# Deferring the tanh and gates of the last two feed-forward chunks into the attention stage

## The chip, the cores and the metric

One core of a Trainium2 chip. The metric is the device time of one execution in microseconds.

## The reference, cut to what matters

```python
xn = layernorm(x)                                   # x: 2048 x 448
q  = xn @ wq                                        # 16 heads of 256
s  = softmax(q k^T / 16) v, heads joined, @ wo      # k, v: the last 512 cached positions, 8 kv heads
g  = silu((gelu(xn @ w_gate) * (xn @ w_up)) @ w_down)   # feed-forward width 1792
out = x + s * g
```

The kernel works on four chunks of 512 rows. It computes the gates `g` of all chunks first, stores them to memory, and fetches them again when the attention output of each chunk is finished. SiLU is written as x * (1 + tanh(x/2)) with factors folded elsewhere, so it can use tanh beside the softmax's exp.

## The kernel before

Every operation is recorded into one list; each engine gets its operations in the recorded order, and a helper inserts the semaphore waits that buffers and data demand. So the place of a line in the program decides its place in an engine's queue. The down product of chunks 1 to 3 is a Strassen-like scheme of seven half-size products (`down7`): PE makes the products, DVE adds them up, ACT takes tanh, DVE multiplies.

```python
def down7(c, banks, g, b_g, order=(3, 6, 5, 4, 2, 1), then=None):
    B1, B4, B6, B7, B5, B3 = banks
    ...
    product(0, B1, A(0, 0))
    act(U2, bank[B1][:, 0:D], ACT.Copy, (b_ps[B1],), bU2, scale=F)
    for j in order:
        product(j, *what[j], j != 1)
    if then:
        then()                        # chunk 2: the differences that chunk 3 needs, on DVE
    plus(U2, bU2, B6, U2, bU2)        # plus: one DVE pass, bank * F + V
    plus(U3, bU3, B7, U2, bU2)
    sums(0, B4, U3, bU3)              # sums: a plus, then tanh on ACT
    sums(1, B5, U3, bU3)
    gate(0, 1, 0)                     # gate: (tanh + 1) * sum on DVE
    plus(U2, bU2, B5, U2, bU2)
    act(Cs[2][0][:, :], bank[B1][:, 0:D], ACT.Copy, (b_ps[B1],), (Cs[2][1],), scale=F)
    sums(2, B3, U2, bU2)
    gate(1, 1, 1); store(1)
    sums(3, None, None, None)
    gate(2, 0, 1)
    ...                               # gate(3), store(0)
```

The attention loop interleaves with it. `s_mm` puts a head's four score products on PE, their exponentials on ACT, their normalisation on DVE (`pn`) and their transposes on the DMA queue of SP (`pT`). `pv` is the product with the values, two heads later.

```python
for m in range(NS):                   # heads of all chunks
    if m in groups:                   # query products for the next 4, 8 or 6 heads, two heads at a time
        ...
        if m == Q0 and p == 0:        # Q0 = 4: the second query group
            K.reuse(b_kT[2:] + b_va[3:])
        if p == 0 and m in (Q0, Q0 + QS):
            for g in range(2, 7) if m == Q0 else (7,): load_k(g)
            for g in range(3, 6) if m == Q0 else (6, 7): load_v(g)
    s_mm(m)
    if m == 0: down7(2, ...)()        # after the first head's scores
    if m == 1:
        down7(3, ...)()               # after the second head's scores
        ...
        for t in range(NG2): load_g2(t)                                # POOL: first gate tiles
        for t in range(NXR): dma("pool", xr[:, t, :], x_view[:, t, :], ...)   # POOL: first input tiles
    if len(late) == LAG: pv(late.pop(0))
```

The scores use the banks AB0 to AB3, the value products BB0 to BB3, and `down7` borrows AB2, AB3 and all of BB.

The softmax here doesn't subtract the row's maximum and nothing guards it: scores larger than these inputs give would overflow.

## Time and profile before

| | before |
|---|---|
| time, median | 546.23 us |
| span of the profiled run | 544.4 us |
| PE busy | 537.4 us, 99% |
| PE idle in 114 to 156 us | 2.2 us |

The lines are shown in the prediction. Two habits of reading help here. A line of the waits view is "engine line waited for: us in total, times, longest us". And on PE, compare the starts of equal groups rather than their ends: a group of eight attention matmuls is listed with 1.89 us, but the next group starts 1.73 us after it. The Trainium skill warns of matmul busy time too: "Perfetto Trace Analysis", section "Identifying the Most-Contended Engine", calls it no good measure of how close a kernel is to the roofline, because PE's instructions are pipelined.

### The profile page before, as it was taken

To read this page: it belongs to the slowest core of one execution; us is meant where nothing else is said; L and a number is where in the kernel's file an instruction comes from. 1 tells how busy PE (TensorE), PEld (TensorE's weight loads), DVE (VectorE), ACT (ScalarE), POOL (GpSimd) and SP (SyncE) were. 2 spreads that over 40 slices of the span, in tenths; PEclk is the share of its full clock that TensorE was granted. 3 is DMA by queue.
4 is the path that set the end of the run, shared out by engine and by line. 5 is a ranking of instruction groups with operands and counts; after the bars stand their busy time and mean duration, and the time that the engine had idled before them with its cause. 6 is when DMAs were issued, how large, how long until landed. Compare 5 with 4: busy or idle time off the path is not lost.

```text
span 544.4 us, 10795 instructions
## 1 busy us (share of the span) xinstructions
PE 537.4 (99%) x4106; PEld 305.8 (56%) x4106; DVE 376.1 (69%) x823; ACT 313.9 (58%) x784; POOL 39.5 (7%) x78
## 2 busy tenths in 40 slices
PE   9999999999999999999999999999999999999997
PEld 5554457458644444894444469644444984444487
DVE  6673885799757757944775786467667934776775
ACT  5433854873648858306875870388488216876820
POOL 1130400000100000003001000020000003001010
PEclk9999999999999999999999999999999999999999
DMA  9569272912398758302771680056456402783631
GB/s 283 132 185 130 48 138 71 293 40 53 106 177 196 144 115 155 79 1 67 165 152 33 152 155 1 18 139 155 95 102 151 68 1 75 162 151 84 151 51 34
DMA packets 171459, 61.36 MB, mean 113 GB/s; under 512 B 154960, under 2 KB 168272, under 8 KB 171408
## 3 DMA queue, kind: packets, MB, share of 16 engines
q1 hardware_dynamic: 167632, 51.39, 44.4%
q0 software_dynamic: 3008, 8.72, 7.1%
q8 instruction: 32, 0.52, 0.4%
q10 hardware_dynamic: 768, 0.57, 0.3%
q14 instruction: 19, 0.16, 0.1%
HBM read 19.76 MB, written 3.67 MB: 43 GB/s over the span
## 4 chain that ended last, share of the span: by engine, by line
PE 90%; DVE 5%; ACT 2%; issue 1%; DMA 1%; DVEq 0%; ACTq 0%
PE bank L390 89%; ACT p L836 2%; DVE wt L384 1%; DVE pn L843 1%; DMA pT<-pn 1%; DVE actTh L557 1%; PE bank L507 1%; DVE qT L821 0%; DVE sd L384 0%; DVE rden L840 0%; DVE cd L608 0%; DVE tmp L608 0%; ACT th L381 0%; DVE actTh L384 0%; PE bank L488 0%
## 5 line engine op out<-in xcount | busy, mean ns | idle before, releaser
L836 ACT ACTIVATE p<-bank 128x512 f32<-128x512 f32 x256 | 150.4, 596 | 26.3 <-DVE pn L843 24.0
L390 PE MATMUL bank<-kT,qT 128*128 128x512 bf16 x512 | 121.6, 380 | 1.1 <-ACT p L836 1.1
L390 PE MATMUL bank<-pT,va 128*128 128x512 bf16 x512 | 120.8, 379 | 0.0
L843 DVE TENSOR_SCALAR pn<-p,rden 128x512 bf16<-128x512 f32 x256 | 113.0, 484 | 9.5 <-DMA pT<-pn 5.1
L390 PE MATMUL bank<-xnT,wq 64*128 64x512 bf16 x768 | 94.9, 377 | 0.5 <-DVE oTh L861 0.5
L390 PEld LDWEIGHTS bank<-kT,qT 128*128 128x128 bf16 x512 | 49.0, 98 | 63.8 <-issue 3.4
L390 PE MATMUL bank<-xnT,wgu 64*128 64x512 bf16 (+2 forms) x768 | 84.2, 351 | 0.1
L390 PEld LDWEIGHTS bank<-pT,va 128*128 128x128 bf16 x512 | 49.8, 98 | 60.7 <-DMA pT<-pn 1.6
L381 ACT ACTIVATE qT<-bank 128x512 bf16<-128x512 f32 x76 | 44.1, 596 | 55.0 <-PE bank L390 53.4
L821 DVE CAST qT<-bank 128x512 bf16<-128x512 f32 x52 | 34.9, 690 | 51.4 <-PE bank L390 51.4
L390 PEld LDWEIGHTS bank<-xnT,wq 64*128 64x128 bf16 x768 | 36.6, 94 | 47.0 <-ACT p L836 2.0
L390 PEld LDWEIGHTS bank<-xnT,wgu 64*128 64x128 bf16 x768 | 37.1, 95 | 36.9 <-issue 0.6
L840 DVE RECIPROCAL rden<-rsum 128x2 f32<-128x2 f32 x128 | 21.2, 166 | 48.3 <-ACT p L836 48.2
L836 ACT ACTIVATION_READ_ACCUMULATOR p<-bank 128x1 f32 x256 | 51.7, 202 | 0.0
L381 ACT ACTIVATE gl<-bank 128x512 bf16<-128x512 f32 x56 | 33.2, 597 | 29.5 <-PE bank L390 27.0
L390 PE MATMUL bank<-wt,sr 128*128 128x224 f16 x512 | 49.7, 259 | 0.0
L390 PEld LDWEIGHTS bank<-wt,sr 128*128 128x128 f16 x512 | 49.1, 98 | 0.0
L381 ACT ACTIVATE xnT<-bank 128x224 bf16<-128x224 f32 (+2 forms) x12 | 4.4, 400 | 72.2 <-PE bank L390 70.9
L861 DVE TENSOR_SCALAR oTh<-bank 128x512 f16<-128x512 f32 x62 | 42.4, 683 | 0.0
L381 ACT ACTIVATE oTh<-bank 128x512 f16<-128x512 f32 x66 | 38.9, 589 | 4.6 <-PE bank L390 4.6
L390 PE MATMUL bank<-wt,oTh 128*128 128x224 f16 x384 | 38.3, 259 | 0.3 <-ACT oTh L381 0.3
L390 PEld LDWEIGHTS bank<-wt,oTh 128*128 128x128 f16 x384 | 36.7, 98 | 1.8 <-ACT oTh L381 1.1
(77 smaller groups left out, 407.9 us busy)
## 6 DMA issues: line engine op xcount, KB each, us to landing
wtb<-in_A_wo_dram POOLq DMA_DIRECT2D x4, 896.0 KB, 10.8
wq<-in_A_wq_dram SPq DMA_DIRECT2D x2, 1536.0 KB, 7.3
va<-in_A_v_cache_dram SPq DMA_DIRECT2D x8, 256.0 KB, 4.1
pT<-pn SPq DMA_TRANSPOSE x128, 2.8
xr<-in_A_x_dram POOLq DMA_DIRECT2D x15, 112.0 KB, 2.3
wd<-in_B_w_down_dram SPq DMA_DIRECT2D x1, 1568.0 KB, 7.6
g<-g_all POOLq DMA_DIRECT2D x14, 112.0 KB, 2.3
out_dram<-xr POOLq DMA_DIRECT2D x12, 112.0 KB, 2.1
```

Of the source, the lines that this page charges most:

```text
L381: K.op("act", lambda e, o=o, i=i: e.activation(o, i, func, scale=scale), reads, writes)
L384: K.op(eng, lambda e: e.tensor_tensor(o, x, y, op), reads, writes)
L390: ins = e.matmul(o, lhsT=l, rhs=r, start=st, stop=sp, skip_group_check=True)
L507: ins = e.matmul(bank[b][:, 0:w], lhsT=gl[:, 0, 0:P], rhs=gl[:, 0, 0:w], start=True, stop=True)
L557: K.op("dve", lambda e: e.tensor_tensor(o[:, c % 2, f, :], bank[b + 1], gl[:, s, :], ALU.mult), (b_ps[b + 1], b_gl[s]), (b_actT[c % 2][f],))
L821: K.op("dve", lambda v, s=s, b=b: v.tensor_copy(qT[:, s, 1, :], bank[b + 1]), (b_ps[b + 1],), (b_qT[s][1],))
L836: K.op("act", lambda e, b=b, r=r, z=z: e.activation(p32[:, z, :], bank[b], ACT.Exp, scale=att_scale, accum_out=rsum[:, r:r + 1]), (b_ps[b] ...
L840: K.op("dve", lambda e, r=r: e.reciprocal(rden[:, r - 1:r + 1], rsum[:, r - 1:r + 1]), b_rsum[r - 1:r + 1], b_rden[r - 1:r + 1])
L843: K.op("dve", lambda e, r=r - 1 + t, z=(n - 1 + t) % NP32, y=y, t=t: e.tensor_scalar(pn[:, y, t, :], p32[:, z, :], rden[:, r:r + 1], None, ...
L861: K.op("dve", lambda v, i=i, b=b: v.tensor_scalar(oTh[:, i, :], bank[b], WS, None, op0=ALU.mult), (b_ps[b],), (b_oT[i],))
```

## The change

The intent: take the tanh and gates of chunks 2 and 3 out of the way of the first heads' exponentials. The sums stay where they are and are kept in buffers. Chunk 2's tanh and gates run while PE makes chunk 3's products, chunk 3's run between pairs of the second query group. To free memory for the kept sums, chunks 2 and 3 get one tanh buffer instead of two, key and value loads are split by what each has to wait for, and POOL's first five loads move behind chunk 3's gates. One product of chunk 2 changes its turn, and chunk 1's tanh and gates now follow all its sums. `K.reuse` says that the buffers named take over memory of others, so that their first writer waits for the last users of those. Cut to its core:

```diff
+            outs = [(x[:, :], [bx]) for x, bx in Cs[:2]] + [(U3, bU3)] + [(Cs[2][0][:, :], [Cs[2][1]])]
             ...
             sums(0, B4, U3, bU3)
             sums(1, B5, U3, bU3)
-            gate(0, 1, 0)
+            act(outs[3][0], bank[B1][:, 0:D], ACT.Copy, (b_ps[B1],), outs[3][1], scale=F)
             plus(U2, bU2, B5, U2, bU2)
-            act(Cs[2][0][:, :], bank[B1][:, 0:D], ACT.Copy, (b_ps[B1],), (Cs[2][1],), scale=F)
             sums(2, B3, U2, bU2)
-            gate(1, 1, 1)
-            store(1)
-            sums(3, None, None, None)
-            gate(2, 0, 1)
-            def end():
-                gate(3, 0, 0)
-                store(0)
+            def end(*qs):
+                for q in qs: tanh(q)
+                for q in qs:
+                    gate(q)
+                    if q in (1, 3): store((0, 1)[q == 1])
             return end
 ... second query group
+                    if m == Q0 and p < 3:
+                        K.reuse(b_kT[2:6] + b_va[3:4] if p == 0 else b_kT[6:] + b_va[4:] if p == 2 else [])
+                        for k in ((2, 3, 4, 5), (), (6,))[p]: load_k(k)
+                        if p == 0: load_v(3)
+                        if p < 2:
+                            gates3(2 * p); gates3(2 * p + 1)
+                        else:
+                            load_v(4); load_v(5)
+                            K.reuse([b for y in b_xr for b in y])
+                            for t in range(NG2): load_g2(t)
+                            for t in range(NXR): dma("pool", xr[:, t, :], x_view[:, t, :], (), b_xr[t])
 ... after the first and second head's scores
-                    down7(2, ..., g2w, b_g2w, then=lambda: [sum_act(3, k) for k in range(4)])()
+                    gates2 = down7(2, ..., g2w, b_g2w, (3, 4, 6, 5, 2, 1), lambda: [sum_act(3, k) for k in range(4)])
-                    down7(3, ..., (3, 4, 2, 5, 6, 1))()
+                    gates3 = down7(3, ..., (3, 4, 2, 5, 6, 1), lambda: [gates2(q) for q in range(4)])
 ... (buffer places and the old load lines cut)
```

More of the change, by code (lines that the diff above doesn't have):

```diff
@@ L344, in bass_recurrent_scan__sliding_block_cached__geglu_ffn__prompt_kernel @@
         a_v, a_th = b_va[3].lo, at2 + 3 * TD
-        dn[2] = places(2, [(2, a_v), (1, a_v + SD), (0, b_pT[2][0].lo)], [a_v + 2 * SD, b_pT[1][0].lo, b_pn[2].lo], [a_th, b_pT[1][0].lo + CD])
-        dn[3] = places(3, [], [a_v + 2 * SD, b_pT[2][0].lo, b_pn[2].lo], [a_th, b_pT[2][0].lo + CD])
+        dn[2] = places(2, [(2, a_v), (1, a_v + SD), (0, b_pT[2][0].lo)],
+                       [a_v + 2 * SD, b_pT[2][0].lo, b_pT[2][0].lo + CD], [a_th])
+        dn[3] = places(3, [], [a_v + 2 * SD, a_v + SD, a_v + SD + CD], [a_th])
         dn[3][0].update({i: (actTh[:, 0, 0:NH, i * HC // 2:i * HC // 2 + HC], b_actT[0][0:NH]) for i in (0, 2)})
@@ L609, in plus, with tanh, gate @@
                     out=o, in0=bank[b][:, 0:D], scalar=F, in1=V, op0=ALU.mult, op1=ALU.add), [b_ps[b]] + bV, bo)
+            outs = [(x[:, :], [bx]) for x, bx in Cs[:2]] + [(U3, bU3)] + [(Cs[2][0][:, :], [Cs[2][1]])]
             def sums(q, b, V, bV):
-                x, bx = Cs[(0, 1, 0, 2)[q]]
-                if b is not None:
-                    plus(x[:, :], [bx], b, V, bV)
-                y, by = Ts[q % 2]
-                act(y[:, :], x[:, :], ACT.Tanh, (bx,), (by,), scale=0.5)
-            def gate(q, r, n):
+                plus(*outs[q], b, V, bV)
+            def tanh(q):
+                x, bx = outs[q]
+                y, by = Ts[q % len(Ts)]
+                act(y[:, :], x, ACT.Tanh, bx, (by,), scale=0.5)
+            def gate(q):
+                r, n = ((1, 0), (1, 1), (0, 1), (0, 0))[q]
                 two = lambda x: x.rearrange("p (t d) -> p t d", t=2)
-                (x, bx), (y, by) = Cs[(0, 1, 0, 2)[q]], Ts[q % 2]
+                (x, bx), (y, by) = outs[q], Ts[q % len(Ts)]
                 K.op("dve", lambda e: e.scalar_tensor_tensor(
-                    out=g[r][:, :, n * N2:(n + 1) * N2], in0=two(y[:, :]), scalar=1.0, in1=two(x[:, :]),
-                    op0=ALU.add, op1=ALU.mult), (by, bx), b_g[2 * r:2 * r + 2])
+                    out=g[r][:, :, n * N2:(n + 1) * N2], in0=two(y[:, :]), scalar=1.0, in1=two(x),
+                    op0=ALU.add, op1=ALU.mult), [by] + bx, b_g[2 * r:2 * r + 2])
             def store(r):
@@ L633, in down7 @@
                 product(j, *what[j], j != 1)
+            K.reuse([b for _, b in Cs + Ts])
             if then:
@@ L639, in down7 @@
             sums(1, B5, U3, bU3)
-            gate(0, 1, 0)
+            act(outs[3][0], bank[B1][:, 0:D], ACT.Copy, (b_ps[B1],), outs[3][1], scale=F)
             plus(U2, bU2, B5, U2, bU2)
-            act(Cs[2][0][:, :], bank[B1][:, 0:D], ACT.Copy, (b_ps[B1],), (Cs[2][1],), scale=F)
             sums(2, B3, U2, bU2)
-            gate(1, 1, 1)
-            store(1)
-            sums(3, None, None, None)
-            gate(2, 0, 1)
-            def end():
-                gate(3, 0, 0)
-                store(0)
+            def end(*qs):
+                for q in qs:
+                    tanh(q)
+                for q in qs:
+                    gate(q)
+                    if q in (1, 3):
+                        store((0, 1)[q == 1])
             return end
@@ L790, in bass_recurrent_scan__sliding_block_cached__geglu_ffn__prompt_kernel @@
                 if DOWN_AT[n + 1] == 1:
-                    down7(1, (cur[0], cur[0] + 1, cur[1], cur[1] + 1, nxt[0], nxt[0] + 1),
-                          (g2x[:, 0:2, :], g2x[:, 2:4, :]), b_g2x)()
+                    end = down7(1, (cur[0], cur[0] + 1, cur[1], cur[1] + 1, nxt[0], nxt[0] + 1),
+                          (g2x[:, 0:2, :], g2x[:, 2:4, :]), b_g2x)
+                    end(0, 1)
+                    end(2, 3)
                     cur, nxt = (nxt[1], cur[1]), (cur[0], nxt[0])
@@ L999, in bass_recurrent_scan__sliding_block_cached__geglu_ffn__prompt_kernel @@
                         sum_act(2, 2 + p)
-                    if m == Q0 and p == 0:
-                        K.reuse(b_kT[2:] + b_va[3:])
-                    if p == 0 and m in (Q0, Q0 + QS):
-                        for g in range(2, 7) if m == Q0 else (7,):
-                            load_k(g)
-                        for g in range(3, 6) if m == Q0 else (6, 7):
-                            load_v(g)
+                    if m == Q0 and p < 3:
+                        K.reuse(b_kT[2:6] + b_va[3:4] if p == 0 else b_kT[6:] + b_va[4:] if p == 2 else [])
+                        for k in ((2, 3, 4, 5), (), (6,))[p]:
+                            load_k(k)
+                        if p == 0:
+                            load_v(3)
+                        if p < 2:
+                            gates3(2 * p)
+                            gates3(2 * p + 1)
+                        else:
+                            load_v(4)
+                            load_v(5)
+                            K.reuse([b for y in b_xr for b in y])
+                            for t in range(NG2):
+                                load_g2(t)
+                            for t in range(NXR):
+                                dma("pool", xr[:, t, :], x_view[:, t, :], (), b_xr[t])
+                    if m == Q0 + QS and p == 0:
+                        load_k(7)
+                        load_v(6)
+                        load_v(7)
                     if end and p:
@@ L1017, in bass_recurrent_scan__sliding_block_cached__geglu_ffn__prompt_kernel @@
                 if m == 0:
-                    down7(2, (BB[0], BB[1], AB[2], AB[3], BB[2], BB[3]), g2w, b_g2w,
-                          then=lambda: [sum_act(3, k) for k in range(4)])()
-                    K.reuse(b_pT[1] + b_pn[2:])
-                else:
-                    K.reuse(dn[3][3])
-                    down7(3, (BB[1], BB[0], AB[2], AB[3], BB[2], BB[3]), g2w, b_g2w, (3, 4, 2, 5, 6, 1))()
+                    gates2 = down7(2, (BB[0], BB[1], AB[2], AB[3], BB[2], BB[3]), g2w, b_g2w, (3, 4, 6, 5, 2, 1),
+                                   lambda: [sum_act(3, k) for k in range(4)])
+                else:
+                    gates3 = down7(3, (BB[1], BB[0], AB[2], AB[3], BB[2], BB[3]), g2w, b_g2w, (3, 4, 2, 5, 6, 1),
+                                   lambda: [gates2(q) for q in range(4)])
+                    K.reuse(b_pT[2])
                 if m == LAG - 1:
-                    K.reuse(b_pT[2] + b_pn[2:])
                     K.reuse(b_oT + [b for y in b_qT[:QS - Q0] for b in y])
                     assert not CASTS and not SUMS
-                    K.reuse([b for y in b_xr for b in y])
-                    for t in range(NG2):
-                        load_g2(t)
-                    for t in range(NXR):
-                        dma("pool", xr[:, t, :], x_view[:, t, :], (), b_xr[t])
             if len(late) == LAG:
```

## The prediction

> **What bounds the kernel now.** I read the page first, then the waits of the matmul engine inside the stage that the diff touches, and last that stage's timelines for PE, ACT and DVE side by side. The page settles how large the answer can be:
>
> ```profile
> span 544.4 us, 10795 instructions
> PE 537.4 (99%) x4106; PEld 305.8 (56%) x4106; DVE 376.1 (69%) x823; ACT 313.9 (58%) x784; POOL 39.5 (7%) x78
> PE 90%; DVE 5%; ACT 2%; issue 1%; DMA 1%; DVEq 0%; ACTq 0%
> ```
>
> PE shows only 7.0 us of idle time in the whole span, and the change removes no matmul. Cut into five stretches, the same trace puts 1.2 us of that idle time into the first 20 us, nothing into 20 to 114, 2.2 us into 114 to 156 (39.81 busy of 42), practically nothing into 156 to 500 and 3.2 us into the tail after 500. The diff acts on the third stretch: the sums, tanh and gates of chunks 2 and 3, wedged between the first attention heads.
>
> In that stretch PE waited for two things:
>
> ```profile
> PE bank L390 <- ACT p L836: 1.7, 3, 0.9
> PE bank L390 <- DVE oTh L861: 0.5, 1, 0.5
> ```
>
> The idle column understates the loss, because a matmul's modelled end includes the time its result takes to come out. Starts against the normal spacing are the better ruler. The PE timeline:
>
> ```profile
> 122.14 1.50 PE L390 MATMUL bank<-wdt,actTh 128*128 128x224 f16 x14
> 124.17 1.51 PE L390 MATMUL bank<-wdt,actTh 128*128 128x224 f16 x14 [0.53 <-ACT p L836]
> ...
> 143.74 1.89 PE L390 MATMUL bank<-pT,va 128*128 128x512 bf16 x8
> 146.51 1.76 PE L390 MATMUL bank<-kT,qT 128*128 128x512 bf16 x6 [0.89 <-ACT p L836]
> 148.53 0.61 PE L390 MATMUL bank<-kT,qT 128*128 128x512 bf16 x2 [0.26 <-ACT p L836]
> 148.97 1.89 PE L390 MATMUL bank<-pT,va 128*128 128x512 bf16 x8
> 150.79 0.82 PE L390 MATMUL bank<-xnT,wq 64*128 64x512 bf16 x6
> ...
> 155.37 0.82 PE L390 MATMUL bank<-xnT,wq 64*128 64x512 bf16 x6 [0.51 <-DVE oTh L861]
> ```
>
> Undisturbed, 14 gate matmuls take 1.35 us (124.17 to the next group at 125.52), eight attention matmuls 1.73 us (142.01 to 143.74), and a query matmul 0.108 us (18 of them, 156.24 to 158.18). So the losses are: at 124.17, 2.03 - 1.35 = 0.68; at 146.51, 2.77 - 1.73 = 1.04; within the scores after it, 2.46 - 1.73 = 0.73; the next head's product 1.82 - 1.73 = 0.09; and 36 query matmuls from 150.79 to 155.37, 4.58 - 3.89 = 0.69. **Sum: 3.23 us.** That is what is to be had.
>
> Why PE waited there is in the ACT timeline:
>
> ```profile
> 144.77 1.11 ACT L381 ACTIVATE th<-cd 128x448 f32<-128x448 f32 x2 [0.98 <-DVE cd L608]
> 145.79 0.58 ACT L836 ACTIVATE p<-bank 128x512 f32<-128x512 f32 x1
> ```
>
> The scores of the third head began at 142.01, so their first bank was full by about 142.5; ACT reached its exponential only at 145.79, because four tanh stood before it in ACT's queue, with gaps of 4.10 and 0.98 us in which they waited for DVE sums. The fourth head's scores need those banks back. The 5.55 us transfer in the chain of waits is the other half: the transposed weights issued at 148.18 shared the DMA with five loads that POOL issued from 147.69 to 150.4, against a median landing of 2.8 us; DVE then sat 2.07 us, and its copy out of a bank came late for the query product at 155.37.
>
> **What the Trainium skill says.** "PSUM — Partial Sum Buffer", section "Engine vs sequencer instructions": the ACT and DVE queues are strictly first in, first out. The trace agrees: the exponential's input stood ready some 3.3 us while it waited behind tanh. "ScalarE: Activation LUTs", section "Table sets: the hidden batching unit": tanh sits in the same table set as exp, so spreading tanh among exponentials should cost no table load. The trace agrees: the one load (1.28 us) of this stage is at 113.77, and none stands between tanh and exp later. "VectorE: DVE Perf Modes", section "Why PSUM operands drop a tier": a PSUM operand leaves fp32 at the plain rate. The sums and the gates both take 622 ns for 448 columns whether they read PSUM or not, so moving a gate does not change its cost. "DMA: Bandwidth & Descriptors", section "Issuing engines are not separate DMA queues": loads from POOL and SP share the 16 engines; the 5.6 us landing against 2.8 agrees.
>
> **The change part by part.** No matmul, sum, tanh or gate is added or removed: eight sums-and-copies, four tanh (about 0.53 us each) and four gates (0.62) per chunk as before. Only places, buffers and transfers move.
>
> 1. Product order of chunk 2. The product whose left side is an already finished difference now runs before the one that needs the last score bank. Its input was finished at 120.6 and its bank evacuated by 119.7, so it can start at 123.49; the one that waited then starts at 124.84, after the exponential that held it to 124.17. Gain 0.68 us on PE. The chunk-3 differences on DVE overwrite an input of that product, now free at about 126.2 instead of 125.5; DVE gets there at 126.2, so this is even or 0.1 us.
>
> 2. Chunk 2's tanh and gates leave the place before the second head's exponentials. These, which ran at 135.03, can begin at about 130.8, as soon as their scores exist. The six sums run on DVE from 129.5 to 133.2 unbroken, then the four normalisations of the second head to about 135.7. Freed banks are enough for what follows.
>
> 3. They then run behind chunk 3's first copy on ACT. One tanh buffer makes them a ping-pong: tanh 0.66 to the gate's start, gate 0.67 to the next tanh, 1.33 us a round (142.26 to 142.92 in the trace gives the first). Four rounds from 135.0 end at about 140.3. This is 5.3 us in which DVE is held, and chunk 3's sums can start only then.
>
> 4. Chunk 3's sums: 140.3 to 144.0 by six sums of 0.55 to 0.65. PE, 0.68 ahead, starts the third head's scores at 141.3. Their third and fourth banks are needed at 142.2 and 142.6; the sums release them at about 141.0 and 141.6. That fits with about 1.0 us to spare. ACT is then free, so the exponentials start at about 142.0, the fourth waits for a normalisation at 144.6, and the next scores (PE at 144.8, last bank needed at 146.1) find the bank read by 145.2. So 1.04 + 0.73 + 0.09 = 1.86 us come back.
>
> 5. Chunk 3's tanh and gates go between query pairs. A pair takes PE 3.03 us. ACT holds 1.25 us of copies and two tanh of 1.11, DVE 1.34 and two gates of 1.16: 2.4 and 2.5 us, both under 3.03, and the banks are wanted a pair later. No cost.
>
> 6. POOL's five loads move behind the gates, out of the transposes' way. The bank copy that held the query product should end near 150.5, needed at 152.1: 0.69 us back.
>
> Sum: 0.68 + 1.86 + 0.69 = 3.23, and 546.23 - 3.23 = 543.0. I leave 0.1 us for small slips: **543.1 us**, 0.6% less. After the query group PE has no idle time in which a shift could be lost. Chunk 1, where all tanh now follow all sums, ends its gates about 1 us later, but DVE has gaps of 0.9 us there, and PE waited for nothing between 20 and 114: zero.
>
> **The rivals.** First, the ping-pong delays the chunk-3 sums: if a round costs 1.6 instead of 1.33 us, the sums slip 1.1 us and the scores' third bank comes late; the stall at 146.5 would move to 142 and part of the 1.86 us would be lost, time near 543.8. For it: tanh and gate wait for each other through one buffer. Against it: the measured 0.66 and 0.67 already contain the semaphore times.
>
> Second, the transfers only collide elsewhere. The key loads now start near 151 instead of 156, but the last of them and the five POOL loads wait for gates at about 157 to 158 and are in flight to about 163, when the fifth head's transposes are issued. Should those land in 5.5 us again, DVE waits about 0.5 us, perhaps twice; the cost on PE would be 0 to 0.7 us. Against it: right after the key loads, at 166.72, the transposes of before went out with no wait on PE.
>
> Third, PE's idle time was harmless slack and ACT or DVE sets the pace of the attention that follows, giving the gain back. ACT's period there is 3.45 us per head (164.32 to 167.83 to 171.28), PE's 3.46. That is close, and it speaks for caution, but the pace of PE is unbroken from 156 to 500, so a start 3.2 us earlier should end 3.2 us earlier. Full loss would leave 546.2.
>
> **Range and chances.** The ceiling of the gain is 3.23 us plus perhaps 0.5 that I overlooked, so 542.5 is the low end. Rivals one and two together would cost up to 1.5 us: the high end is 544.6. Two per cent is 10.9 us, more than all idle time of PE, so faster by that much is ruled out by the count of matmuls; slower by that much would take a serial wait that no view suggests.
>
> **What would show it.** Right: PE busy stays 537 us while the span drops to about 541.2; the waits of PE on exponentials and on the bank copy in 114 to 156 are gone; the fifth head's scores start near 160.4 instead of 163.67; second-head exponentials begin near 131; the transposes of the third head land in about 3 us. Wrong at step 1: a gap before the fourth product group remains. Wrong at step 3 or 4: a wait of PE on a sum (or on the bank copy) appears near 142. Wrong at step 6: a transpose with 5 us landing near 163 and a DVE wait behind it. A time above 545 would mean that the lost time was taken back within the attention stage.

## The result and the profile after

Four executions of each: 544.34 us median (543.65 to 544.61) against 546.21 us (544.96 to 546.40). Ratios here are from the runs of both kernels in the same rounds, and not quite the ratio of the quoted medians: 0.9969, 95% interval 0.9951 to 0.9986. The time fell by 1.9 us, where the prediction had 3.1: inside its range, within 2% as forecast, but with little more than half of the gain.

The page after, the lines that answer to those of before:

```profile
span 542.4 us, 10788 instructions
PE 536.5 (99%) x4106; PEld 305.8 (56%) x4106; DVE 375.8 (69%) x823; ACT 313.8 (58%) x784; POOL 39.6 (7%) x78
PE 93%; ACT 2%; DVE 2%; DMA 2%; issue 1%; ACTq 0%
```

The span is 2.0 us shorter at the same work; DVE's share of the chain that ended last fell from 5% to 2%, while the share of DMA rose from 1% to 2%. PE's waits from 112 to 185 us after the change, the whole answer:

```profile
PE bank L391 <- DMA pT<-pn: 0.9, 1, 0.9
```

The two waits of before (on exponentials, on a bank copy) are gone. A new one stands there: the product with the values waits for transposed weights. The PE timeline shows where:

```profile
123.35 1.50 PE L391 MATMUL bank<-wdh,sd 128*128 128x224 f16 x14
124.69 1.50 PE L391 MATMUL bank<-wdt,actTh 128*128 128x224 f16 x14
...
142.90 1.89 PE L391 MATMUL bank<-pT,va 128*128 128x512 bf16 x8
144.63 1.89 PE L391 MATMUL bank<-kT,qT 128*128 128x512 bf16 x8
146.35 1.89 PE L391 MATMUL bank<-pT,va 128*128 128x512 bf16 x8
148.18 0.82 PE L391 MATMUL bank<-xnT,wq 64*128 64x512 bf16 x6
...
160.37 1.90 PE L391 MATMUL bank<-kT,qT 128*128 128x512 bf16 x8
...
167.29 1.89 PE L391 MATMUL bank<-kT,qT 128*128 128x512 bf16 x8
170.08 1.90 PE L391 MATMUL bank<-pT,va 128*128 128x512 bf16 x8 [0.91 <-DMA pT<-pn]
```

Up to 160.37 every group starts at its normal spacing: the fifth head's scores begin at 160.37, where the prediction said "near 160.4 instead of 163.67". Then 2.79 us pass between two starts where 1.73 is normal: 1.06 us are given back. Comparing the starts of equal query groups along the whole run, the lead over the kernel before is 3.30 us in the second query group (0.14 of it from ahead of the first head), 2.22 in the third (189.84 against 192.06), 2.07 at 342.78, 1.85 at 382.93 and 2.04 at 483.60. So most of what is missing is lost in one place, near 168; some 0.4 us more goes between there and 383, and 0.2 comes back. The traces show where: at 275.44 and 363.18 a product with the values starts 0.14 and 0.22 us late after a weight load that waited 0.5 us for a transpose, and at 466.55 the kernel before has the same.

Two more views of the profile after show what happened near 168. First the DMA issues of POOL, then a line of DVE, and the landing times of the transposes from 160 to 180 us (issue to landing, minimum, median, maximum):

```profile
161.74 1.10 POOL L376 DMA_DIRECT2D g<-g_all  x2 [94.00 <-DMA g_all<-g]
162.83 1.83 POOL L376 DMA_DIRECT2D xr<-in_A_x_dram  x3
```

```profile
169.44 0.88 DVE L850 TENSOR_SCALAR pn<-p,rden 128x512 bf16<-128x512 f32 x2 [2.00 <-DMA pT<-pn]
```

```profile
DMA to landing us min/median/max: 2.7/2.7/5.8
```

And from the chain that ended last, the transfer that PE waited for:

```profile
165.21 4.82 DMA pT<-pn
```

POOL's five loads go out from 161.7 to 164.7, as soon as chunk 3's gates are stored. The fifth head's transposes are issued from 163.5. The longest lands 5.8 us after its issue, where 2.7 is the median, and the one that PE needs after 4.82 us. DVE waits for a buffer of weights, and PE for the weights. It is the collision that the kernel before had at 148, moved to 163.

### The profile page after: what moved, and what is told of

It reads as the page before. It is cut to its first block, busy times and chain, and to the rows that moved or that the text cites. A ratio compares the mean times of both kernels' runs of the same rounds, so it can differ in the third digit from the quotient of the medians.

```text
span 542.4 us, 10788 instructions
## 1 busy us (share of the span) xinstructions
PE 536.5 (99%) x4106; PEld 305.8 (56%) x4106; DVE 375.8 (69%) x823; ACT 313.8 (58%) x784; POOL 39.6 (7%) x78
## 4 chain that ended last, share of the span: by engine, by line
PE 93%; ACT 2%; DVE 2%; DMA 2%; issue 1%; ACTq 0%
PE bank L391 92%; ACT p L843 2%; DMA pT<-pn 2%; DVE pn L850 1%; PE bank L508 1%; DVE rden L847 0%; ACT qT L382 0%; PE bank L489 0%; ACT oTh L382 0%; ACT xnT L382 0%; DVE xnT L385 0%; DVE xr L385 0%; DVE gl L421 0%; DVE epst L422 0%; ACTq L155 0%
## 5 line engine op out<-in xcount | busy, mean ns | idle before, releaser
L391 PE MATMUL bank<-pT,va 128*128 128x512 bf16 x512 | 120.9, 379 | 1.0 <-DMA pT<-pn 0.9
L391 PE MATMUL bank<-kT,qT 128*128 128x512 bf16 x512 | 121.0, 379 | 0.0
L391 PE MATMUL bank<-xnT,wq 64*128 64x512 bf16 x768 | 94.9, 376 | 0.0
L391 PEld LDWEIGHTS bank<-pT,va 128*128 128x128 bf16 x512 | 49.7, 98 | 62.0 <-DMA pT<-pn 3.4
L391 PEld LDWEIGHTS bank<-kT,qT 128*128 128x128 bf16 x512 | 49.4, 98 | 61.7 <-issue 3.4
L391 PE MATMUL bank<-xnT,wgu 64*128 64x512 bf16 (+2 forms) x768 | 83.8, 350 | 0.2
L391 PEld LDWEIGHTS bank<-xnT,wq 64*128 64x128 bf16 x768 | 36.7, 94 | 46.3 <-ACT p L843 2.1
L391 PEld LDWEIGHTS bank<-xnT,wgu 64*128 64x128 bf16 x768 | 36.8, 94 | 37.2 <-issue 0.6
L391 PE MATMUL bank<-wt,sr 128*128 128x224 f16 x512 | 49.7, 259 | 0.0
L391 PEld LDWEIGHTS bank<-wt,sr 128*128 128x128 f16 x512 | 49.1, 98 | 0.0
L391 PE MATMUL bank<-wt,oTh 128*128 128x224 f16 x384 | 38.3, 259 | 0.3 <-ACT oTh L382 0.3
L391 PEld LDWEIGHTS bank<-wt,oTh 128*128 128x128 f16 x384 | 36.7, 98 | 1.8 <-ACT oTh L382 1.1
```

The lines of the kernel that those rows point to most:

```text
L391: ins = e.matmul(o, lhsT=l, rhs=r, start=st, stop=sp, skip_group_check=True)
```

## The experiments

All kernels gave correct results. To compare traces, I use the distance from the start of the first head's scores to that of the fifth head's: before 163.67 - 119.06 = 44.61 us, changed 160.37 - 118.92 = 41.45 us. What happens ahead of the first head (some 0.1 us of jitter) drops out. The starts in the traces, two of the kernel before (L390) and the first of the changed one (L391):

```profile
119.06 1.90 PE L390 MATMUL bank<-kT,qT 128*128 128x512 bf16 x8
163.67 1.90 PE L390 MATMUL bank<-kT,qT 128*128 128x512 bf16 x8
118.92 1.90 PE L391 MATMUL bank<-kT,qT 128*128 128x512 bf16 x8
```

In the traces of all the later runs whose distance is given, the first record of both groups is missing (x7 where there should be x8). Both starts are then those of second matmuls, and the distance stays the same.

### POOL's loads held back

The edit adds a dependency, since moving the lines alone would not delay a queue with nothing else in it:

```diff
+                    if m == Q0 + QS and p == 1:           # third query group
+                        hold = [K.ops[-1]]
+                        K.reuse([b for y in b_xr for b in y])
+                        for t in range(NG2): load_g2(t, hold)
+                        for t in range(NXR): dma("pool", xr[:, t, :], x_view[:, t, :], (), b_xr[t], hold)
 ... and the same lines removed from the second group
```

> POOL's five loads (two gate tiles, three input tiles) held back until the third query group, about 45 us later. Theory A (these loads slow the fifth head's transposes): the transposes issued near 163.5 land in about 3 us instead of 4.8 to 5.8, DVE's 2.0 us wait and PE's 0.9 us wait near 168 to 170 are gone, and the product after the seventh head's scores starts at about 169.0 instead of 170.08; time about 1.1 us under the changed kernel, 543.3. Theory B (the key, value and gate-store transfers of SP that are still in flight slow them): nothing changes, 544.3. Theory C (the lead gained earlier is slack that is taken back by another wait): the wait near 168 goes, and another of about 1 us appears before 250 us.

Measured: 542.73 us median of four executions (542.87 with the slow one counted), ratio to before 0.9943 (0.9931 to 0.9956). One of five executions, the profiled one, took 1149 us: its matmuls ran at half their pace or slower throughout (fourteen matmuls of a down product took 2.7 to 2.9 us instead of 1.35), at a recorded clock of 1.0. It is left out, and its cause stays open. So the kernel was run again for its profile.

> The kernel with POOL's loads held until the third query group once more, since its profile fell into an execution of 1149 us. Theory A: no wait of PE on a transpose in 160 to 172 us, the product after the seventh head's scores near 169.0, the transposes of that stretch within about 3 to 4 us (SP's key and value loads still overlap the first), time near 542.9. If instead that wait stays at 0.9 us in the profile, the faster time has another cause.

Measured: 542.86 us (542.47 to 542.90), ratio 0.9940 (0.9928 to 0.9952), no slow execution. The PE timeline of this run, and the landing times of its transposes from 160 to 180 us:

```profile
167.05 1.89 PE L391 MATMUL bank<-kT,qT 128*128 128x512 bf16 x8
168.78 1.89 PE L391 MATMUL bank<-pT,va 128*128 128x512 bf16 x8
```

```profile
DMA to landing us min/median/max: 2.7/2.7/3.8
```

The spacing is 1.73 us again, the longest landing 3.8. The distance to the fifth head is 41.44 us, equal to that of the changed kernel: nothing before 160 moved, only the loss near 168 went. The five loads of POOL, at the place where the change has them, are shown to be what kept the gain down. This version beats the kernel before by some 3.1 us. With the changed kernel it shared no rounds; the ratios to before are 0.9940 and 0.9969, and their intervals just touch.

### SP's loads late instead

```diff
-                        for k in ((2, 3, 4, 5), (), (6,))[p]: load_k(k)
+                        for k in ((2, 3, 4, 5), (), ())[p]: load_k(k)
-                            load_v(4); load_v(5)
 ...
             s_mm(m)
+            if m == Q0 + 3:
+                load_v(4); load_v(5); load_k(6)
```

> The opposite half: the last key load and two value loads of SP put behind the eighth head's transposes, POOL's loads left where the change has them. Theory A: PE still waits 0.9 us near 170, time 544.3 within noise. Theory B: the transposes land in about 3 us, the wait is gone, about 543.3.

Measured: 544.29 us, ratio 0.9971 (0.9958 to 0.9984), no better than the change. The wait near 169 shrank to 0.43 us and the longest landing to 4.7 us, so SP's transfers have a share in it; but two new waits on transposes stood at 183.94 (0.57 us) and 187.79 (0.22 us), after the moved loads had gone out from 176.9. The three sum to 1.2 us. How much of the 1.06 us SP's loads cost beside POOL's is therefore known only from this one trace.

### Both late

> Both halves late. Theory A: as with POOL's loads late alone, about 543.3. Theory B: as with SP's loads late alone. If each of the two contributes, only this one lands every transpose of 160 to 172 us in about 3 us and brings the full 1.06 us, while the two single moves bring a part each.

Measured: 543.83 us, ratio 0.9965 (0.9953 to 0.9977). Between 160 and 172 all is clean, the product after the seventh head's scores starts at 168.94. But now one longer wait follows the moved loads:

```profile
184.93 1.90 PE L391 MATMUL bank<-pT,va 128*128 128x512 bf16 x8 [2.02 <-DMA pT<-pn]
```

Neither theory had this: three SP loads sent among the transposes of steady attention cost 2.0 us in this execution, while the same loads in the query group cost nothing measurable once POOL's are away. The profiled execution (544.88 us) was the slowest of the five; the others, at 543.8 to 543.9, took about 1 us less and were not profiled. Here the place for loads was where no transpose is due, not merely "later".

### POOL's loads doubled

```diff
                             for t in range(NG2): load_g2(t)
                             for t in range(NXR): dma("pool", xr[:, t, :], x_view[:, t, :], (), b_xr[t])
+                            for t in range(NG2): load_g2(t)
+                            for t in range(NXR): dma("pool", xr[:, t, :], x_view[:, t, :], (), b_xr[t])
```

> Every one of POOL's five loads issued twice at the same place (the second writes the same data). Theory A: the fifth head's transposes land later still, in some 7 us, and PE's wait near 170 grows from 0.9 to about 2 to 3 us: 545.5 to 546.5. Theory B or C: the wait stays at 0.9 us and the time at 544.3.

Measured: 547.54 us median (544.84 to 548.45), ratio to before 1.0019 (0.9998 to 1.0040). In the profiled execution (545.25 us) PE waited 2.07 us where the change has 0.91, the longest landing was 6.3 us. The second five went out later than the first, two at 165.6, one at 166.9 and two at 169.9, so the load on the DMA did not quite double at once. The wait moved as Theory A has it, at the low end of its 2 to 3 us. The median went beyond my 546.5: four of six executions ran at a mean granted clock of 0.996 or 0.997 and took 546.7 to 548.5 us, the other two at 0.999 and 1.0 took 545.3 and 544.8. None of the four was profiled, but the next run's profile fell into such an execution.

### The old product order

```diff
-  down7(2, ..., (3, 4, 6, 5, 2, 1), ...)
+  down7(2, ..., (3, 6, 5, 4, 2, 1), ...)
```

> The changed kernel with chunk 2's products in their old order. My step 1: the 0.68 us gap before the third product (at 123.5 to 124.2) returns, everything after it starts 0.68 us later, the fifth head's scores at about 161.05 instead of 160.37; time 0.7 us above the changed kernel, 545.0. Rival: the gap is only moved, later waits absorb it, and the fifth head's scores start at 160.4 all the same.

Measured: the distance to the fifth head is 161.05 - 118.91 = 42.14 us, 0.69 more than with the new order, as step 1 has it. The time is inconclusive: 545.70 us median, but from 543.66 to 548.58, ratio 0.9994 (0.9970 to 1.0018). In the profiled execution, 547.76 us, the collision was worse than usual. The wait, and the stretches of the trace around it (from:to length, PE busy, and so on; the third figure from the end is PE's granted clock):

```profile
171.98 2.75 PE L391 MATMUL bank<-pT,va 128*128 128x512 bf16 x8 [2.35 <-DMA pT<-pn]
174.53 1.06 PE L391 MATMUL bank<-kT,qT 128*128 128x512 bf16 x2
```

```profile
170.00:172.00 2.00, 0.02 (x1) 0.03 (x2) 1.55 (x4) 1.27 (x4) 0.00 (x0) 1.00 1.29 198
172.00:174.00 2.00, 2.00 (x7) 0.80 (x8) 1.58 (x5) 1.18 (x3) 0.00 (x0) 0.72 0.72 161
174.00:176.00 2.00, 1.78 (x5) 0.76 (x5) 1.04 (x2) 0.32 (x1) 0.00 (x0) 0.50 0.82 187
176.00:178.00 2.00, 2.00 (x10) 0.82 (x9) 0.72 (x3) 1.67 (x7) 0.00 (x0) 0.93 0.34 76
```

After 2.35 us without a matmul PE's clock was halved for some 3 us, and the eight matmuls that follow took 2.55 us to the next start instead of 1.73, the next eight 2.60. So the late transfer cost twice here: 2.51 us at the wait, 1.7 us by the clock. The sum, 4.2 us, is what separates this execution from the 543.54 us of the run after this one. A loss of 1.7 us of clock in a span of 545.9 is a mean clock of 0.997, so the other executions at 0.996 or 0.997 have probably met the same; they were not profiled.

### The old product order, with POOL's loads late

> POOL's loads late and the old product order of chunk 2: the same undoing as before, where the collision cannot blur it. My step 1: the gap of 0.68 us is back, fifth head's scores at 161.05 instead of 160.37, no wait near 170, 543.5 against 542.9. Rival: absorbed, 542.9.

Measured: 543.54 us (543.28 to 543.92), ratio 0.9961 (0.9949 to 0.9973) against 0.9940 with the new order. Distance 161.07 - 118.93 = 42.14 us against 41.44. With the collision gone the undoing can be read in the time: 0.7 us by the medians (1.1 by the ratios, which come from different rounds), not absorbed.

### Only the new order, on the kernel before

> The kernel before with nothing but the new order of chunk 2's products. My step 1 alone: the gap at 124.17 is gone, but the third head's exponentials still stand behind tanh. If the chain of tanh and sums starts as much earlier as the products end (0.68 us), the fifth head's scores start at about 163.0 and the time is 545.5; if that chain hangs on DVE's differences (ending 129.5 whatever PE does) only as far as chunk 3's last product allows, the gain shows in full, and otherwise the wait on the exponentials grows by up to 0.68 us and the time stays at 546.2.

Measured: 544.93 us, ratio 0.9981 (0.9969 to 0.9993). Distance 163.14 - 119.31 = 43.83 us, 0.78 less than before. The stall behind the exponentials kept its length (0.89 us of idle time, as before) and moved forward with the products. The gain shows in full; the 0.1 us above 0.68 is the wait on the bank copy, 0.42 us where it was 0.51.

### Only POOL's loads late, on the kernel before

> The kernel before with only POOL's five loads held until the third query group. My step 6 alone: the four transposes from 148.18 land in about 3 us instead of up to 5.6, DVE's 2.07 us wait and PE's 0.51 us wait on a bank copy at 155.37 go, the fifth head's scores start near 163.0 instead of 163.67, time 545.5. Rival: the transposes are slow because four of them come at once with the gate stores (Theory B), and nothing changes.

Measured: 545.01 us (544.95 to 545.23), ratio 0.9983 (0.9971 to 0.9995).

```profile
162.89 1.67 PE L390 MATMUL bank<-kT,qT 128*128 128x512 bf16 x7 [0.16 <-ACT qT L381]
```

Distance 162.89 - 118.96 = 43.93 us, 0.68 less than before; the wait on the bank copy is gone, the longest landing of the four transposes 3.6 us. So 0.7 us of the predicted gain could be had without the change's main idea.

### Chunk 3's gates back in their place

On the kernel with POOL's loads late:

```diff
                     gates3 = down7(3, ..., lambda: [gates2(q) for q in range(4)])
+                    for q in range(4): gates3(q)
 ... and the calls in the second query group removed
```

> POOL's loads late (542.9) and chunk 3's tanh and gates put back straight after chunk 3's sums, so that only chunk 2's are deferred. My steps 3 to 5: the four rounds of tanh and gate (1.33 us each) then stand on ACT before the third head's exponentials, which start near 147.4 instead of 141.8; PE waits some 3.3 us at the fourth head's scores: fifth head's scores near 163.8 instead of 160.4, time about 546.2, more if the clock drops after so long a gap. Rival: the banks are free early enough anyway, and the time stays at 542.9.

Measured: 547.53 us median, ratio 1.0037 (1.0025 to 1.0049), slower than before. PE waited for the exponentials:

```profile
147.68 3.47 PE L391 MATMUL bank<-kT,qT 128*128 128x512 bf16 x8 [3.08 <-ACT p L843]
```

```profile
146.00:148.00 2.00, 0.32 (x1) 0.13 (x2) 1.06 (x2) 1.53 (x4) 0.00 (x0) 0.87 0.34 115
148.00:150.00 2.00, 2.00 (x6) 0.71 (x5) 1.33 (x5) 1.83 (x7) 0.00 (x0) 0.50 0.34 115
```

The fourth head's scores start 3.29 us later than with the deferral (144.39), 3.3 was expected; the rest, up to a distance of 46.27 us (4.83 more), falls where the clock is down. The deferral of chunk 3 is what allows one tanh buffer: in their old place its four rounds hold up the fourth head. This is not the kernel before, which had two tanh buffers and its tanh between the sums; so the 4.83 us is what this version needs the deferral for, not what the deferral gained.

### Chunk 2's gates back in their place

```diff
                     gates2 = down7(2, ...)
+                    for q in range(4): gates2(q)
 ... and taken out of chunk 3's place
```

> POOL's loads late and chunk 2's tanh and gates straight after chunk 2's sums, so that only chunk 3's are deferred. If deferring chunk 2's is needed for the gain, as my steps 2 and 3 have it, a wait of PE of about 1 us or more appears at the second or third head and the time is 544 or more. Rival: DVE's chain from 129.5 to 143.5 is the same work in another order, the sums of chunk 3 end at about 143.7 as before, and the time stays within 0.3 us of 542.9: the deferral of chunk 2 is then worth nothing by itself.

Measured: 544.15 us (543.91 to 544.30), ratio 0.9972 (0.9959 to 0.9985), distance 161.91 - 118.92 = 42.99 us, 1.55 more than with both deferred. The rival falls: the order on ACT and DVE does matter. The wait stands at a place that I had not named, inside chunk 3's products:

```profile
138.45 2.86 PE L391 MATMUL bank<-wdt,actTh 128*128 128x224 f16 x28 [1.37 <-ACT p L843]
```

The products that borrow AB2 and AB3 need the second head's exponentials to have read them. With chunk 2's tanh first, these exponentials start at 136.57 instead of 130.75. Here too one buffer stands in for two: the kernel before had these exponentials at 135.03 and no wait of PE at these products.

### The changed kernel again

> The changed kernel itself once more beside these, for its spread: 544.3, PE's wait on a transpose near 170 of about 1 us, its length following the transposes' landing (4.8 to 5.8 us).

Measured: 543.96 us median of six, ratio 0.9981 (0.9959 to 1.0003). The profiled execution lost 0.89 us near 168 (0.74 us as idle time, longest landing 5.7 us). The six lie at 543.28, 543.31, 543.39, 544.52, 545.86 and 547.48, the last at a mean clock of 0.997. With POOL's loads late, five executions lay within 0.43 us, four within 0.90. So the kernel with the collision also spreads more. The clock is not all of it: the execution of 545.86 us had a mean clock of 1.0, and was not profiled.

## Why the prediction was right, point by point

| part | predicted | shown by | measured |
|---|---|---|---|
| 1. product order | 0.68 us | undone twice, done alone | 0.69, 0.70, 0.78 us |
| 2 to 4. tanh and gates away from the exponentials | 1.86 us | the whole less the other two | 1.7 to 1.8 us |
| 5. gates in the query group | 0 | PE busy 15.00 of 15.00 us in 141 to 156, 4.00 of 4.00 in 156 to 160 | 0 |
| 6. POOL's loads away from the transposes at 148 | 0.69 us | done alone | 0.68 us |
| sum up to the fifth head | 3.23 us | 44.61 - 41.45 | 3.16 us |
| slips, later collision | 0.1 us | trace of the changed kernel | 1.06 us near 168, some 0.2 net later |

- Steps 1 to 6 held, with times. The four tanh of chunk 2 ran at 134.86, 136.22, 137.49 and 138.75, rounds of 1.26 to 1.36 us where I had 1.33; chunk 3's sums began at 139.91 (I had 140.3), the third head's exponentials at 141.81 (142.0).
- With one tanh buffer both halves of the deferral are needed: taking back either one costs 1.55 or 4.83 us by the distance to the fifth head. No run shares out the gain of 1.7 to 1.8 us between the halves. Step 2 was right about its times (130.75, it had 130.8) but did not name the wait that it prevents, that of chunk 3's products for AB2 and AB3.
- The first rival, a slower ping-pong, did not come. The third, that the gain is slack for PE, fell too: with the collision gone, the whole 3.1 us arrive at the end. (Its reading of ACT's period was loose: the first of the two steps that it names is 3.51 us, not 3.45.)
- The second rival came, and the term that failed is its size. The prediction named it, "0 to 0.7 us", and left 0.1 us in the sum for it. The transposes landed late as described, at the time described (issued at 163.5), but DVE waited 2.00 us once, where the prediction had "about 0.5 us, perhaps twice", and PE lost 1.06 us in the profiled run (0.89 in the other one). One step of its timing was wrong: it has POOL's loads wait for gates at 157 to 158 and in flight to about 163. POOL in fact waited for the stores of these gates to land, and sent its loads from 161.7 to 164.7, beside the transposes and not ahead of them. That this lag is what made the cost larger is likely, but no run tests it. The argument "right after the key loads the transposes of before went out with no wait on PE" was not to the point: at 166.72 in the kernel before, POOL's loads had landed long ago, so that trace had never shown the two together.
- The gain was 1.9 us instead of 3.1, inside the range only because the range allowed for this rival and the first together. With its 0.7 us for this rival alone the prediction would have ended at 543.8, below the 544.34 measured; that the room left for a rival that did not come covered the rest is luck.

## What to carry to other kernels

When a transfer is tied to a buffer that a change frees later, work out what else is on the DMA at its new time, and give it an explicit dependency that puts it where no transfer with a waiting consumer is due. A deferral pays where the queue that it leaves blocks something and the queue that it joins has room in each period; here both were worked out from the durations of a trace to within 0.2 us, and only the collision of transfers was not. And undo the parts one by one: here a fifth of the available gain came from one product's turn, and another fifth could be had by moving five loads.

## What the Trainium skill lacked or had wrong

- "TensorE: Matmul & The Clock Gate", section "HAM oscillation — how this bites in real kernels": it warns of idle gaps above about 3.4 us. Here a gap of 2.35 us was followed by a granted clock of 0.72 and 0.50 over the next 2 us stretches, one of 3.08 us by 0.50, while gaps of 2.07 and 2.02 us left the clock at 1.00. No run here tests what decides it.
- "DMA: Bandwidth & Descriptors", section "Issuing engines are not separate DMA queues": it says that transfers from all engines interleave, and that is what was seen, but gives no figure for what a short transpose suffers. With SP's last key and value loads alone near it the longest landing was 3.8 us, against a median of 2.7; with POOL's five loads of 112 KB beside them it was 5.7 to 5.8 us, with those sent twice 6.3 us.
- "ScalarE: Activation LUTs", section "Table sets: the hidden batching unit": it puts a table load at about 2.7 us. The trace of the changed kernel has three, of 1.28 us each. That tanh among exponentials needs no further load agrees: the last of the three stands at 113.64, before the first of those tanh.
- No page gives a cause for a whole execution at about half its pace with a recorded clock of 1.0, as the one of 1149 us. The nearest is the warning in "TensorE: Matmul & The Clock Gate", section "Seeing it yourself", that recorded clock events can be unreliable; no run here checks it.
